# Sixteen plain steps on two tiles at a time, at the start of a Fourier-mixing and ELU kernel

## The chip, the cores and the metric

The kernel runs on one core of a Trainium2 chip. The metric is the device time of one execution in microseconds (us), as the median of several runs. A core has five engines that run side by side, each in the order of its own program: TensorE (PE, matrix products into PSUM; PEld is its loading of weights), VectorE (DVE), ScalarE (ACT), GpSimd (POOL) and SyncE (SP), which issues most of the DMA transfers. They wait for one another by semaphores.

## The reference

```
X = np.fft.fft(x, axis=1)            # x: (8, 3008, 256) float32
X = np.fft.fft(X, axis=2).real       # -> 24064 tokens x 256
h = X @ w_in                         # w_in: (256, 2048) float64
g = np.where(h > 0, h, np.exp(np.minimum(h, 0)) - 1)
out = (g @ w_out).astype(np.float32) # w_out: (2048, 256) float64
```

The weights reach the kernel as 64-bit words, and it makes 32-bit floats of them itself.

## The kernel before

**Transforms.** The Fourier transform over the 3008 positions is done as matrix products with cosine and sine matrices (`MC`), on sums and differences of four quarters of a batch (the folds, `fold_x`). `Dft` writes the results into rings of columns in SBUF: `Rr` and `Ir` for real and imaginary parts, `Rb` for one more channel, spread over all partitions. The second transform, over the 256 channels, is folded into the first weight matrix: `fold_chunk` multiplies 256 columns of w_in by channel matrices, `put_chunk` (ScalarE) copies the results to `Wc` and `Ws`, and `spread_last_row` sends one row of `Ws` through DRAM (`wx`, L392) and back as columns (`wex`, L394).

**Steps.** The main loop has 376 steps: 47 tiles of 256 columns, with 8 steps each. Step i takes 256 of the 2048 hidden features, those of chunk i % 8. `mm_P` makes the real part's product (tile `H`), `even_part` adds the extra channel with `wex` (tile `E`, VectorE, L713), `mm_Q` adds the imaginary part to `H`; `h_minus` makes 2E - H, the mirrored position; ScalarE and VectorE make the ELU of both (`G`, L723, L739). Two steps later the second product follows, into the accumulators pA to pD. In a plain step (`mm_plain`, the first 8) these are 8 matmul instructions. In all later steps they are 7, by a Winograd scheme: POOL makes four sums of blocks of `G` (`sum_1` to `sum_4`, L362), and four sums of weights (`WT`, `sum_weights`) take the place of part of the weights. At the end of a tile VectorE combines the accumulators (`COMB`), transposes them (L888, L895) and SyncE stores them (`store`, L927).

**Order.** All operations are written into a list of events with a time each (`at(t, fn)`, L1017; one slot is `PERIOD` = 4.8 in these units, called T). Sorted by these times, the list gives the order on the engines. The times are an order only: nothing is delayed until then. DMA issues aren't held to that order, so SyncE's order follows the scheduler. A transfer waits for the one issued eight places before it, by its semaphore.

**Start.** The weights are read in 8 chunks of w_in and 8 of w_out, 512 KB each (class `Chunk`). `load` brings the 64-bit words to a home in SBUF that something else uses later (`IN_HOMES`, `OUT_HOMES`: the homes of `WT`, parts of `Wc`, `Ws` and `w2`, `xl`, `rx`, `ot`). `fields` (VectorE) cuts out exponent and mantissa, `power` (ScalarE) makes the power of two in a temporary, `round` adds the two halves of the mantissa and `scale` multiplies. A chunk that is `shared` has the conversions on ScalarE (two more passes in `power`) and the addition and multiplication on POOL (`gtt`); the others do these on VectorE. In the kernel before, slots 0 to 4 have up to two chunks each, since step i needs chunk i of w_in from slot i on:

```
(w1_chunks[3], 0, 0), (w2_chunks[0], 0, 1), (w1_chunks[4], 1, 0),
(w2_chunks[1], 1, 1), (w1_chunks[5], 2, 0), (w2_chunks[2], 2, 1),
```

**The last channel.** One channel of all batches goes a way of its own: `load_ext` (L563) copies it from x in 16 parts, element by element; L580 writes rows to DRAM (`xe_dr`), `get_ext` (L586) reads them back (`xs`), `fold_ext` (POOL) folds them into `xe`, and `dft_ext` transforms them on TensorE, at slot 25 of the list. `dft_ext_0` and `ext_rows(1, gtt, 1)` do one part for batch 0 alone, earlier. `load_x(b)` (L144, L153, L154) loads a batch's four quarters, two of them by POOL.

Of the kernel before, what the change touches and what calls it, by code (L numbers as in the profile page):

```python
# [9 lines left out]
FP = mybir.dt.float32  # L10
BF = mybir.dt.bfloat16
U32 = mybir.dt.uint32
I32 = mybir.dt.int32
# [64 lines left out]
def kernel(  # L78
# [94 lines left out]
    class Chunk:  # L173
# [29 lines left out]
        def fields(self):  # L203

            if not wide:
                return
            lo, hi, dst = self.parts()
            if self.tmp_tag in ACC:
                t = bank(self.tmp_tag).bitcast(I32)
            else:  # L210
                t = spool.tile([128, 512], I32, tag=self.tmp_tag, bufs=1, name="pow2")
            self.t = t.rearrange("p (a b) -> p a b", a=dst.shape[1])
            pin(
                nc.vector.tensor_scalar(
                    out=self.t, in0=hi, scalar1=0x7FF00000, scalar2=None,
                    op0=ALU.bitwise_and,
                )
            )
            pin(
                nc.vector.tensor_scalar(  # L220
                    out=dst.bitcast(I32), in0=hi, scalar1=0xFFFFF, scalar2=0x100000,
                    op0=ALU.bitwise_and, op1=ALU.bitwise_or,
                )
            )
# [47 lines left out]
    def w1_dst(c):  # L272
        q, half = divmod(c, 2)
        if q not in w1:
# [3 lines left out]

    IN_HOMES = [(f"WT{c}", 1, 1024) for c in range(4)] + [
        Wc[:, 1024:2048],  # L280
        Ws[:, 1024:2048],
        ("xl0", 1, 6 * ND),
        ("xl1", 1, 6 * ND),
    ]
    OUT_HOMES = [w2[:, 1024 * (c + 1) : 1024 * (c + 2)] for c in range(3)] + [
        ("xl2", 1, 6 * ND),
        ("xl3", 1, 6 * ND),
        ("rx", 1, HALF + 1),
        ("ot", 2, 1024),
        ("ot", 2, 1024),  # L290
    ]
    ACC = ("pA", "pB", "pC", "pD")
    IN_TMP = ("u", "v", "u", "v", "pC", "pD", "pC", "pD")
    OUT_TMP = ("u", "v", "u", "v", "u", "pC", "pD", "pC")
    w1_chunks = [
        Chunk(
            moe_w_in[:, c * 256 : (c + 1) * 256].rearrange("(h p) n -> p h n", p=128),
            lambda c=c: w1_dst(c),
            IN_HOMES[c],
            IN_TMP[c],  # L300
            c in (1, 2, 3),
        )
        for c in range(8)
    ]
# [3 lines left out]
            lambda c=c: w2[:, c * 512 : (c + 1) * 512].rearrange("p (q n) -> p q n", q=2),  # L308
            OUT_HOMES[c],
            OUT_TMP[c],  # L310
            c < 5,
        )
        for c in range(8)
    ]
# [32 lines left out]
    def bank(tag):  # L347
        bufs = 3 if tag == "H" else 1
        return ppool.tile([128, 512], FP, tag=tag, bufs=bufs, name=tag)
# [14 lines left out]
    def act(o, i, func=AF.Copy, **kw):  # L364
        pin(nc.scalar.activation(out=o, in_=i, func=func, **kw))  # L365
# [440 lines left out]
    def mm_plain(i, a):  # L806

        S = steps[i]
        if i == 0 and a == 0:
            tiles[0] = Tile()  # L810
            tiles[0].acc = [bank(t) for t in ACC[0:2]]
        for n, (half, sign) in enumerate(((0, a), (1, 1 - a))):
            for r in range(2):
                mm(
                    tiles[0].acc[a][:, n * TW : (n + 1) * TW],
                    w2b(i, r, half),
                    blk(S, 2 * sign + r),
                    i == 0 and n == 0 and r == 0,
                    i == 7,
                )  # L820
        if a:
            del steps[i]
# [19 lines left out]
    def comb_copy(q):  # L842
        T = tiles[q]
        T.p1 = spool.tile([128, TW], FP, tag="p1", bufs=1, name="p1")
        act(T.p1, T.acc[0][:, 0:TW])

    def plain_u(q):
        T = tiles[q]
        T.u = spool.tile([128, 512], FP, tag="u", bufs=1, name="u")
        act(T.u, T.acc[0])  # L850

    def plain_v(q):
        T = tiles[q]
# [31 lines left out]
    def turn_u(q):  # L885
        T = tiles[q]
        T.o = spool.tile([128, 1024], FP, tag="ot", bufs=2, name="ot")
        pin(nc.vector.transpose(out=T.o[:, 0:512], in_=T.u))  # L888
        store(q, 0, 1, 0)
        store(q, 1, 0, 1)  # L890

    def turn_v(q):
        T = tiles.pop(q)
        tiles[q, 1] = T
        pin(nc.vector.transpose(out=T.o[:, 512:1024], in_=T.v))  # L895
        tiles[q] = T
        store(q, 2, 0, 0)
        store(q, 3, 1, 1)
        del tiles[q], tiles[q, 1]
# [126 lines left out]
    def load_rest():  # L1026

        ops["x1", 0]()
        act(MC[1, 0][0:1, 0:1], L_first[1][0:1, 0:1])
        load_mats(1, 0)  # L1030
        for chunk in (
            w1_chunks[2], w1_chunks[3], w2_chunks[0], w1_chunks[4], w2_chunks[1],
            w1_chunks[5], w2_chunks[5],
        ):
            chunk.load()

    at(-26.0, w1_chunks[0].fields)
# [8 lines left out]
    at(-24.8, lambda: fold_now("c2 e2 E2 o3 o2"))  # L1046
    at(-24.5, begin_x_even)
    at(-24.4, lambda: fold_now("c0 e0 c1 e1 E0 EO0"))
    at(-20.8, w2_chunks[2].load)
    for ri in (0, 1):  # L1050
        at(-20.7, lambda ri=ri: load_mats(ri, 1))
    at(-13.2, lambda: fold_chunk(0))
    at(-13.1, lambda: put_chunk(0))
    at(-13.0, lambda: dft_now(R_even, 1, "pA"))
# [16 lines left out]
    at(-10.5, lambda: dft_now(I_even, 0, "M"))  # L1071
    at(-10.4, w1_chunks[1].round)
    at(-10.3, w1_chunks[1].scale)
    at(0.95, w1_chunks[2].fields)
    at(0.96, w1_chunks[2].power)
    at(0.97, w1_chunks[2].round)
    at(1.7, w1_chunks[2].scale)
    at(1.3, lambda: fold_now("EO1"))
    at(3.9, lambda: fold_now("EO3"))
    at(-1.7, w1_chunks[6].load)  # L1080
    at(-1.6, w1_chunks[7].load)
    at(-1.5, w2_chunks[3].load)
    at(-1.4, w2_chunks[4].load)
    at(1.2, lambda: nc.sync.dma_start(out=pick, in_=PK_dr.ap()))

    T = PERIOD
    for chunk, k, second in (
        (w1_chunks[3], 0, 0),
        (w2_chunks[0], 0, 1),
        (w1_chunks[4], 1, 0),  # L1090
        (w2_chunks[1], 1, 1),
        (w1_chunks[5], 2, 0),
        (w2_chunks[2], 2, 1),
        (w1_chunks[6], 3, 0),
        (w2_chunks[3], 3, 1),
        (w1_chunks[7], 4, 0),
        (w2_chunks[4], 4, 1),
        (w2_chunks[5], 5, 1),
        (w2_chunks[6], 6, 1),
        (w2_chunks[7], 7, 1),  # L1100
    ):
        t = k * T + (1.9 if second and k == 0 else 1.0 if second or k == 0 else -0.5)
        at(t, chunk.fields)
        at(t + 0.02, chunk.power)
        at(t + 0.05, chunk.round)
        at(k * T + (3.7 if second else 1.7), chunk.scale)
    for c in range(1, 8):
        t = (c - 2) * T + 4.7 if c > 1 else 2.3
        at(t, lambda c=c: fold_chunk(c))
        t = (c - 1) * T + 1.4 if c > 1 else 3.0  # L1110
        at(t, lambda c=c: put_chunk(c))
        at(t + 0.01, lambda c=c: spread_last_row(c))
    for i in range(8):
        at((i + 3) * T + 1.0, lambda i=i: sum_weights(i))
    for c, k in ((5, 3.9), (6, 5.6), (7, 6.5)):
        at(k * T, w2_chunks[c].load)
    total = n_tiles * 8
    WINOGRAD = (
        (T + 2.91, sum_1),
# [3 lines left out]
        (2 * T + 0.87, mm_X1),  # L1123
        (2 * T + 3.04, mm_X2),
    )
    for i in range(total):
        t = i * T
        for dt, fn in (
            (0.0, mm_P),
            (0.9, even_part),  # L1130
            (2.17, mm_Q),
            (3.55, h_minus),
            (4.2, below_plus),
            (4.8, below_minus),
            (T + 1.5, exp_plus),
            (T + 2.2, g_plus),
            (T + 2.21, exp_minus),
            (T + 2.9, g_minus),
        ) + (
            (  # L1140
                (2 * T + 0.87, lambda i: mm_plain(i, 0)),
                (2 * T + 3.04, lambda i: mm_plain(i, 1)),
            )
            if i < 8
            else WINOGRAD
        ):
            at(t + dt, lambda fn=fn, i=i: fn(i))
# [4 lines left out]
        (T + 1.0, comb_22),  # L1152
        (T + 2.5, comb_3),
    )
    for q in range(n_tiles):
        t = (8 * q + 9) * T
        for dt, fn in (COMB if q else ((1.45, plain_u), (T + 1.1, plain_v))) + (
            (2 * T + 4.2 if q < n_tiles - 1 else T + 2.4, turn_u),
            (3 * T + 4.2, turn_v),
        ):  # L1160
            at(t + dt, lambda fn=fn, q=q: fn(q))
# [35 lines left out]
    for t, fn in (  # L1197
        (-1.8, I_even.copy),
        (0.0, I_even.plus),
        (0.1, I_even.minus),  # L1200
        (3.1, lambda: dft_now(R_odd, 1, "pA")),
        (3.2, lambda: dft_now(R_odd, 0, "pB")),
        (T + 0.95, R_odd.copy),
        (T + 1.0, R_odd.plus),
        (T + 1.1, R_odd.minus),
        (T + 3.1, lambda: dft_now(I_odd, 1, "pA")),
        (T + 3.2, lambda: dft_now(I_odd, 0, "pB")),
        (2 * T + 0.1, I_odd.copy),
        (2 * T + 0.2, I_odd.plus),
        (2 * T + 0.3, I_odd.minus),  # L1210
    ):
        at(t, fn)
    at(9 * T + 4.75, dft_ext_0)
    for g in (2, 3):
        at(10 * T + 1.46, lambda g=g: ext_side(g, 1))
    at(11 * T + 1.35, lambda: ext_rows(1, gtt, 1))
    at(11 * T + 2.0, lambda: spread_ext(0, 1))
    for n in range(16):
        j, k = divmod(n, 4)
        at(  # L1220
            (12 + 0.75 * n) * T,
            lambda j=j, k=k: load_ext(j, 192 * k, 192 * (k + 1)),
        )
    at(24.4 * T, get_ext)
# [8 lines left out]
    n_big = sum(k[0] not in "czx" for k, _ in fold_keys)  # L1233
    for b in range(1, NB):
        s0 = (b - 1) * steps_b
        l0 = s0 - 8 if b > 1 else 5.2
        at(l0 * T + 0.1, lambda b=b: state.update(L=load_x(b)))
        f0 = max(8, s0 - 1)
        f1 = s0 + 38
        at(f0 * T, lambda b=b: begin_folds(b))  # L1240
        n = 0
        for key in fold_keys:
# [64 lines left out]
```

## Time and profile before

| | |
|---|---|
| median of 6 runs | 1985.47 us (1984.92 to 1986.1) |
| profiled execution | 1995.33 us, span 1993.6 us |
| mean granted TensorE clock | 0.995 |
| busy: PE, PEld | 1960.8 us (98%), 1662.7 us (83%) |
| busy: DVE, ACT, POOL | 1281.0 (64%), 863.0 (43%), 1338.5 us (67%) |
| TensorE pauses before E, xe | 10.0 us (6 times), 7.9 us (once) |

The profile is that of one execution, and its time is longer than the median of the runs. "H<-Rr,Wc x4" is the first product of one step: each matmul instruction on 32-bit floats leaves two records. The line of most TensorE, ScalarE and POOL operations is that of a helper (L353, L365, L362), so they are told apart by their tiles.

### The profile page before, as it was taken

How to read it: one execution, taken by the hardware profiler on the slowest of the kernel's cores; microseconds unless marked ns; L12 is line 12 of the kernel's file. 1: busy time of each engine (PE TensorE's matmuls, PEld its weight loads, DVE VectorE, ACT ScalarE, POOL GpSimd, SP SyncE). 2: the span in 40 equal slices, each digit the busy share in tenths (PEclk: the TensorE clock that was granted, in tenths of full speed). 3: DMA queues.
4: the chain of work that ended last, by engine and by line, in shares of the span. 5: the costliest groups of instructions: out<-in, count | busy, mean ns of one | idle time of the engine just before them, and what ended most of it. 6: DMA issues, size and time to landing. Idle time of an engine off the chain costs nothing.

```text
span 1993.6 us, 26783 instructions
## 1 busy us (share of the span) xinstructions
PE 1960.8 (98%) x8880; PEld 1662.7 (83%) x8880; DVE 1281.0 (64%) x2340; ACT 863.0 (43%) x1654; POOL 1338.5 (67%) x1822
## 2 busy tenths in 40 slices
PE   8998999999999999999999999999999999999998
PEld 4787888888888888888888888888888888888887
DVE  7855656666566666666666665666656665566665
ACT  3543444444444434444434443444434444344443
POOL 3567757787477765777567775677757776455655
PEclk9999999999999999999999999999999999999999
DMA  8238301120001211011101211012010010100101
GB/s 320 85 20 21 87 11 17 28 75 16 15 15 37 59 23 17 14 49 44 26 14 19 59 28 28 12 19 83 12 21 12 19 21 15 17 12 12 22 10 23
DMA packets 256012, 71.61 MB, mean 36 GB/s; under 512 B 244271, under 2 KB 245060, under 8 KB 255362
## 3 DMA queue, kind: packets, MB, share of 16 engines
q1 hardware_dynamic: 251298, 57.05, 15.1%
q0 software_dynamic: 2400, 12.59, 2.0%
q8 instruction: 70, 1.15, 0.2%
q10 hardware_dynamic: 2176, 0.26, 0.1%
q14 instruction: 68, 0.56, 0.1%
HBM read 45.02 MB, written 24.80 MB: 35 GB/s over the span
## 4 chain that ended last, share of the span: by engine, by line
PE 90%; DMA 4%; DVE 2%; SPq 2%; ACT 1%; issue 1%; POOL 0%; DVEq 0%; POOLq 0%; ACTq 0%
PE H L353 36%; PE pB L353 15%; PE pD L353 15%; PE pC L353 15%; PE pA L353 8%; DMA x<-in_x_dram 2%; SPq L563 1%; DMA raw<-in_moe_w_in_dram 1%; DMA xl<-in_x_dram,ix 1%; DVE E L713 1%; DMA out_dram<-ot 0%; DMA wex<-wx 0%; DMA wx<-Ws 0%; SPq L927 0%; DVE G L739 0%
## 5 line engine op out<-in xcount | busy, mean ns | idle before, releaser
L362 POOL TENSOR_TENSOR G<-G 128x256 f32<-128x256 f32 x1472 | 1059.8, 729 | 580.3 <-DVE G L739 466.4
L713 DVE SCALAR_TENSOR_TENSOR E<-Rb,wex,H 128x256 f32<-128x256 f32 x752 | 327.9, 477 | 619.9 <-PE H L353 613.2
L365 ACT ACTIVATE G<-H 128x512 f32<-128x512 f32 x376 | 224.6, 597 | 949.0 <-DVE G L723 949.0
L353 PE MATMUL H<-Ir,Ws 128*128 128x256 f32 x1504 | 388.5, 381 | 10.1 <-DVE E L713 10.0
L353 PE MATMUL H<-Rr,Wc 128*128 128x256 f32 x1504 | 387.3, 380 | 0.7 <-ACT Wc L365 0.7
L353 PE MATMUL pC<-G,WT 128*128 128x256 f32 x1472 | 377.8, 379 | 0.0
L353 PEld LDWEIGHTS H<-Rr,Wc 128*128 128x128 f32 x1504 | 285.5, 190 | 55.0 <-issue 3.1
L353 PEld LDWEIGHTS H<-Ir,Ws 128*128 128x128 f32 x1504 | 277.7, 189 | 60.6 <-DVE E L713 13.4
L353 PEld LDWEIGHTS pC<-G,WT 128*128 128x128 f32 x1472 | 279.7, 190 | 38.0
L723 DVE SCALAR_TENSOR_TENSOR G<-E,H 128x512 f32<-128x512 f32 x376 | 257.4, 684 | 36.4 <-issue 0.6
L739 DVE SCALAR_TENSOR_TENSOR G<-G,H 128x512 f32<-128x512 f32 x376 | 256.2, 681 | 32.3 <-ACT G L365 32.2
L739 DVE SCALAR_TENSOR_TENSOR G<-M,G 128x512 f32<-128x512 f32 x376 | 257.3, 684 | 0.0
L353 PE MATMUL pB<-G,w 128*128 128x256 f32 x800 | 235.4, 381 | 0.0
L353 PE MATMUL pA<-G,w 128*128 128x256 f32 x800 | 234.0, 379 | 0.0
L365 ACT ACTIVATE G<-G 128x512 f32<-128x512 f32 x376 | 233.3, 620 | 0.0
L365 ACT ACTIVATE M<-G 128x512 f32<-128x512 f32 x376 | 224.0, 596 | 0.0
L365 ACT ACTIVATE M<-M 128x512 f32<-128x512 f32 x376 | 221.0, 588 | 0.1
L353 PE MATMUL pD<-G,WT 128*128 128x256 f32 x736 | 219.1, 379 | 1.6 <-DVE v L359 1.6
L353 PE MATMUL pB<-G,WT 128*128 128x256 f32 x736 | 219.3, 380 | 0.8 <-POOL G L362 0.8
L353 PE MATMUL pD<-G,w 128*128 128x256 f32 x736 | 218.9, 379 | 0.0
L353 PEld LDWEIGHTS pB<-G,w 128*128 128x128 f32 x800 | 152.7, 191 | 21.0
L353 PEld LDWEIGHTS pA<-G,w 128*128 128x128 f32 x800 | 152.1, 190 | 20.7
(139 smaller groups left out, 1335.3 us busy)
## 6 DMA issues: line engine op xcount, KB each, us to landing
out_dram<-ot SPq DMA_DIRECT2D x496, 32.0 KB
xl<-in_x_dram SPq DMA_DIRECT2D x16, 768.0 KB
MC<-dft_mats SPq DMA_DIRECT2D x4, 1131.0 KB
out_dram<-ot SPq DMA_DIRECT2D x256, 2.0 KB
Rb<-r SPq DMA_DIRECT2D x10, 376.0 KB
raw<-in_moe_w_in_dram SPq DMA_DIRECT2D x6, 512.0 KB
raw<-in_moe_w_out_dram SPq DMA_DIRECT2D x6, 512.0 KB
out_dram<-ot SPq DMA_DIRECT2D x64, 28.0 KB
```

The costliest lines, as they stand in the source:

```text
L353: nc.tensor.matmul(out_, lhsT=lhsT, rhs=rhs, start=start, stop=stop, skip_group_check=True)
L362: pin(nc.gpsimd.tensor_tensor(out=o, in0=a, in1=b, op=op))
L365: pin(nc.scalar.activation(out=o, in_=i, func=func, **kw))
L563: nc.sync.dma_start(out=t[:, s0:s1], in_=bass.AP(tensor=xt, offset=x.offset + row * ND + 128, ap=[[SEQ * ND, NB], [step * ND, s1 - s0], [1 ...
L713: nc.vector.scalar_tensor_tensor(out=S.E[:, c], in0=Rb[:, cols(i)], scalar=wex[:, f : f + 1], in1=S.H[:, c], op0=ALU.mult, op1=ALU.add,)
L723: nc.vector.scalar_tensor_tensor(out=two(S.G[:, 0:512])[:, :, ::-1], in0=two(S.E), scalar=2.0, in1=two(S.H), op0=ALU.mult, op1=ALU.subtract,)
L739: nc.vector.scalar_tensor_tensor(out=o, in0=e, scalar=-1.0, in1=h, op0=ALU.add, op1=ALU.max)
```

## The change

The first two tiles are taken side by side. Slot 0 does step 0 (tile 0), slot 1 step 8 (tile 1), slot 2 step 1, slot 3 step 9, and so on, up to slot 15; from slot 16 on, slot and step are the same again. Steps 8 to 15 become plain steps; their accumulators are pC and pD. Chunk c of w_in is now first used in slot 2c, and one chunk is converted per slot, in slots 0 to 12 and 14.

Further parts: all chunks but the first of w_in are shared (ScalarE and POOL in place of VectorE); the temporaries of the powers of two, part of them in pC and pD before, all lie in u and v; the homes `Ws`, `xl0` to `xl3` are replaced by `WT0` to `WT3`; the loads are put in another order and more of them later; the sums of weights move from slots 3 to 10 to slots 11 to 16; I_odd's transform moves from the accumulators' banks in slot 1 to H banks in slots 4 and 6; the last channel's early part and its copies move one slot later; tile 0's accumulators, and half of tile 1's, are transposed straight from PSUM, without a copy by ScalarE; batch 1 is loaded and folded on other slots.

```diff
-            if self.tmp_tag in ACC:
-                t = bank(self.tmp_tag).bitcast(I32)
-            else:
-                t = spool.tile([128, 512], I32, tag=self.tmp_tag, bufs=1, name="pow2")
+            t = spool.tile([128, 512], I32, tag=self.tmp_tag, bufs=1, name="pow2")
...
-        Ws[:, 1024:2048],
-        ("xl0", 1, 6 * ND),
-        ("xl1", 1, 6 * ND),
+        ("WT0", 1, 1024),
+        ("WT1", 1, 1024),
+        ("WT2", 1, 1024),
...
-        ("xl2", 1, 6 * ND),
-        ("xl3", 1, 6 * ND),
+        ("WT3", 1, 1024),
+        ("WT0", 1, 1024),
...
-    IN_TMP = ("u", "v", "u", "v", "pC", "pD", "pC", "pD")
-    OUT_TMP = ("u", "v", "u", "v", "u", "pC", "pD", "pC")
+    IN_TMP = "uvvuuuuu"
+    OUT_TMP = "uvvvvvuv"
...
-            c in (1, 2, 3),
+            c > 0,
...
-            c < 5,
+            True,
...
+        q = i // 8
+        if i % 8 == 0 and a == 0:
+            tiles[q] = Tile()
+            tiles[q].acc = [bank(t) for t in ACC[2 * q : 2 * q + 2]]
...
-        pin(nc.vector.transpose(out=T.o[:, 0:512], in_=T.u))
+        pin(nc.vector.transpose(out=T.o[:, 0:512], in_=T.u if q > 1 else T.acc[0]))
...
-        for chunk in (
-            w1_chunks[2], w1_chunks[3], w2_chunks[0], w1_chunks[4], w2_chunks[1],
-            w1_chunks[5], w2_chunks[5],
-        ):
+        w2_chunks[0].load()
+        w1_chunks[2].load()
+        load_mats(0, 1)
+        for chunk in (w1_chunks[3], w2_chunks[1], w1_chunks[4], w2_chunks[2]):
             chunk.load()
...
+        (w2_chunks[0], 0),
+        (w1_chunks[2], 1),
+        (w1_chunks[3], 2),
+        (w2_chunks[1], 3),
+        (w1_chunks[4], 4),
+        (w2_chunks[2], 5),
+        (w1_chunks[5], 6),
+        (w2_chunks[3], 7),
+        (w1_chunks[6], 8),
+        (w2_chunks[4], 9),
+        (w1_chunks[7], 10),
+        (w2_chunks[5], 11),
+        (w2_chunks[6], 12),
+        (w2_chunks[7], 14),
...
     for c in range(1, 8):
-        t = (c - 2) * T + 4.7 if c > 1 else 2.3
+        t = max(2 * c - 3, c % 3) * T + 4.7 if c > 1 else 2.3
         at(t, lambda c=c: fold_chunk(c))
-        t = (c - 1) * T + 1.4 if c > 1 else 3.0
+        t = max(2 * c - 2, 3) * T + 1.4 if c > 1 else 3.0
         at(t, lambda c=c: put_chunk(c))
...
-        at((i + 3) * T + 1.0, lambda i=i: sum_weights(i))
+        at((11 + 0.7 * i) * T + 1.0, lambda i=i: sum_weights(i))
...
-    for i in range(total):
-        t = i * T
+    for slot in range(total):
+        i = slot % 2 * 8 + slot // 2 if slot < 16 else slot
+        t = slot * T
...
-            if i < 8
+            if i < 16
...
+    at(17 * T + 1.0, lambda: turn_u(0))
+    at(17 * T + 4.2, lambda: turn_v(0))
+    at(18 * T + 1.0, lambda: turn_u(1))
+    at(18 * T + 1.45, lambda: plain_v(1))
+    at(19 * T + 4.2, lambda: turn_v(1))
+    for q in range(2, n_tiles):
...
-        (T + 3.1, lambda: dft_now(I_odd, 1, "pA")),
-        (T + 3.2, lambda: dft_now(I_odd, 0, "pB")),
...
+    at_half(4, lambda: I_odd, 1, 0)
+    at_half(6, lambda: I_odd, 0, HALF)
+    at(10 * T + 4.75, dft_ext_0)
...
-            (12 + 0.75 * n) * T,
+            (13 + 0.7 * n) * T,
...
-        l0 = s0 - 8 if b > 1 else 5.2
+        l0 = s0 - 8 if b > 1 else 7.2
...
-        f0 = max(8, s0 - 1)
-        f1 = s0 + 38
+        f0, f1 = (s0 - 1, s0 + 38) if b > 1 else (11, 37)
```

More of the change, by code (lines that the diff above doesn't have):

```diff
@@ L808, in mm_plain @@
         S = steps[i]
-        if i == 0 and a == 0:
-            tiles[0] = Tile()
-            tiles[0].acc = [bank(t) for t in ACC[0:2]]
+        q = i // 8
+        if i % 8 == 0 and a == 0:
+            tiles[q] = Tile()
+            tiles[q].acc = [bank(t) for t in ACC[2 * q : 2 * q + 2]]
         for n, (half, sign) in enumerate(((0, a), (1, 1 - a))):
@@ L814, in mm_plain @@
                 mm(
-                    tiles[0].acc[a][:, n * TW : (n + 1) * TW],
+                    tiles[q].acc[a][:, n * TW : (n + 1) * TW],
                     w2b(i, r, half),
                     blk(S, 2 * sign + r),
-                    i == 0 and n == 0 and r == 0,
-                    i == 7,
+                    i % 8 == 0 and n == 0 and r == 0,
+                    i % 8 == 7,
                 )
@@ L845, in comb_copy @@
         act(T.p1, T.acc[0][:, 0:TW])
[L847 to L850, printed above, removed]
     def plain_v(q):
@@ L894, in turn_v @@
         tiles[q, 1] = T
-        pin(nc.vector.transpose(out=T.o[:, 512:1024], in_=T.v))
+        pin(nc.vector.transpose(out=T.o[:, 512:1024], in_=T.v if q else T.acc[1]))
         tiles[q] = T
@@ L1048 @@
     at(-24.4, lambda: fold_now("c0 e0 c1 e1 E0 EO0"))
-    at(-20.8, w2_chunks[2].load)
-    for ri in (0, 1):
-        at(-20.7, lambda ri=ri: load_mats(ri, 1))
+    at(-20.7, lambda: load_mats(1, 1))
+    at(-20.6, w1_chunks[5].load)
+    at(-20.5, w2_chunks[5].load)
     at(-13.2, lambda: fold_chunk(0))
@@ L1073 @@
     at(-10.3, w1_chunks[1].scale)
[L1074 to L1077, printed above, removed]
     at(1.3, lambda: fold_now("EO1"))
[L1079 to L1083, printed above, removed]
     at(1.2, lambda: nc.sync.dma_start(out=pick, in_=PK_dr.ap()))
     T = PERIOD
[L1087 to L1100, printed above, removed]
+    for chunk, k in (
+        (w2_chunks[0], 0),
[12 more added lines that the diff above has]
+        (w2_chunks[7], 14),
     ):
-        t = k * T + (1.9 if second and k == 0 else 1.0 if second or k == 0 else -0.5)
+        t = k * T + 1.0
         at(t, chunk.fields)
@@ L1105 @@
         at(t + 0.05, chunk.round)
-        at(k * T + (3.7 if second else 1.7), chunk.scale)
+        at(k * T + (3.7 if k else 1.9), chunk.scale)
+    for chunk, t in (
+        (w1_chunks[6], 0.95),
+        (w1_chunks[7], 2.2),
+        (w2_chunks[3], 3.2),
+        (w2_chunks[4], 7.1),
+        (w2_chunks[6], 8.3),
+        (w2_chunks[7], 12.2),
+    ):
+        at(t * T, chunk.load)
     for c in range(1, 8):
-        t = (c - 2) * T + 4.7 if c > 1 else 2.3
+        t = max(2 * c - 3, c % 3) * T + 4.7 if c > 1 else 2.3
         at(t, lambda c=c: fold_chunk(c))
-        t = (c - 1) * T + 1.4 if c > 1 else 3.0
+        t = max(2 * c - 2, 3) * T + 1.4 if c > 1 else 3.0
         at(t, lambda c=c: put_chunk(c))
@@ L1113 @@
     for i in range(8):
-        at((i + 3) * T + 1.0, lambda i=i: sum_weights(i))
-    for c, k in ((5, 3.9), (6, 5.6), (7, 6.5)):
-        at(k * T, w2_chunks[c].load)
+        at((11 + 0.7 * i) * T + 1.0, lambda i=i: sum_weights(i))
+    at(2 * T + 4.2, lambda: fold_now("EO3"))
     total = n_tiles * 8
@@ L1154 @@
     )
-    for q in range(n_tiles):
+    at(17 * T + 1.0, lambda: turn_u(0))
[4 more added lines that the diff above has]
+    for q in range(2, n_tiles):
         t = (8 * q + 9) * T
-        for dt, fn in (COMB if q else ((1.45, plain_u), (T + 1.1, plain_v))) + (
+        for dt, fn in COMB + (
             (2 * T + 4.2 if q < n_tiles - 1 else T + 2.4, turn_u),
@@ L1205 @@
         (T + 1.1, R_odd.minus),
-        (T + 3.1, lambda: dft_now(I_odd, 1, "pA")),
-        (T + 3.2, lambda: dft_now(I_odd, 0, "pB")),
-        (2 * T + 0.1, I_odd.copy),
-        (2 * T + 0.2, I_odd.plus),
-        (2 * T + 0.3, I_odd.minus),
     ):
         at(t, fn)
-    at(9 * T + 4.75, dft_ext_0)
+    at_half(4, lambda: I_odd, 1, 0)
+    at_half(6, lambda: I_odd, 0, HALF)
+    at(10 * T + 4.75, dft_ext_0)
     for g in (2, 3):
-        at(10 * T + 1.46, lambda g=g: ext_side(g, 1))
-    at(11 * T + 1.35, lambda: ext_rows(1, gtt, 1))
-    at(11 * T + 2.0, lambda: spread_ext(0, 1))
+        at(11 * T + 1.46, lambda g=g: ext_side(g, 1))
+    at(12 * T + 1.35, lambda: ext_rows(1, gtt, 1))
+    at(12 * T + 2.0, lambda: spread_ext(0, 1))
     for n in range(16):
```

## The prediction, made before the changed kernel ran

> **What bounds the kernel now.** I read the page first: TensorE is busy for 98% of the span and the chain that ended last is 90% TensorE, at a clock of 0.995. So the time is TensorE's work plus its pauses. The second view is the list of what TensorE waited for over the whole run:
>
> ```profile
> PE H L353 <- DVE E L713: 10.0, 6, 3.5
> PE H L353 <- POOL xe L362: 7.9, 1, 7.9
> PE pA L353 <- DMA MC<-dft_mats: 1.9, 1, 1.9
> PE pD L353 <- DVE v L359: 1.6, 3, 0.5
> ```
>
> Columns: us in total, times, longest. Some 18 us go to two places: the even part E of the first steps, and one wait for `xe`. The third view, TensorE in order of time, places them:
>
> ```profile
> 45.63 2.07 PE L353 MATMUL H<-Ir,Ws 128*128 128x256 f32 x4 [3.51 <-DVE E L713]
> ...
> 74.85 1.13 PE L353 MATMUL H<-Ir,Ws 128*128 128x256 f32 x4 [2.74 <-DVE E L713]
> 75.82 3.25 PE L353 MATMUL pB<-G,w 128*128 128x256 f32 x8
> 78.86 2.27 PE L353 MATMUL H<-w,CC 128*128 128x256 f32 x8
> ...
> 112.46 1.13 PE L353 MATMUL H<-Rr,Wc 128*128 128x256 f32 x4
> ...
> 196.83 4.18 PE L353 MATMUL H<-MC,xe 128*8 128x377 f32 x24 [7.87 <-POOL xe L362]
> 200.94 1.88 PE L353 MATMUL H<-Rr,Wc 128*128 128x256 f32 x4
> ```
>
> Columns: start, length, work, pause before it. A slot runs from one first product (H<-Rr,Wc) to the next. 75.82 also shows a second price: that group takes 3.25 us, later ones 1.89, since the granted clock fell after the pause:
>
> ```profile
> 75.00:78.00 3.00, 3.00 (x10) 2.45 (x11) 2.21 (x4) 2.38 (x6) 1.47 (x3) 0.70 0.65 234
> ...
> 198.00:201.00 3.00, 3.00 (x21) 0.92 (x13) 0.00 (x0) 0.00 (x0) 2.78 (x4) 0.50 1.01 278
> ```
>
> (third number from the end: the clock). The fourth view is SyncE's queue:
>
> ```profile
> 129.32 2.35 SPq L563 DMA_DIRECT2D x<-in_x_dram  x2
> 131.79 7.53 SPq L927 DMA_DIRECT2D out_dram<-ot  x12
> 139.37 10.62 SPq L563 DMA_DIRECT2D x<-in_x_dram  x6
> ...
> 192.55 0.36 SPq L586 DMA_DIRECT2D xs<-xe_dr  x1
> 192.95 8.82 SPq L927 DMA_DIRECT2D out_dram<-ot  x16
> ```
>
> The copies of one channel (L563) come late because tile 0's stores (L927) stand ahead of them; `xs` lands at 194.78, POOL folds it, and TensorE, which was ready at 188.96, starts at 196.83.
>
> **The change part by part.**
>
> *Added products.* A full plain step has 12 matmul instructions, a Winograd step 11. One instruction of 256 columns is two records, and the start-to-start rows give 0.432 us (x8 records every 1.73 us). Steps 8 to 15 turn plain: 8 x 0.432 = 3.5 us more for TensorE.
>
> *Half the weight work per slot.* Before, slots 1 to 4 carry two chunks each; E starts at 44.70, 54.77, 63.88, 73.93 and 82.85, so 9 to 10 us per slot, with VectorE near full. With one chunk, in before's later slots, E starts at 82.85, 89.28, 95.70, 101.58: 6.4, 6.4, 5.9 us. After, one chunk per slot, rounded on ScalarE and POOL. Round trip by rows, start to start: two E 0.79, first field 0.33, three ScalarE passes 0.63+0.56+0.52, two copies of folded weights 0.54, exp 0.52, three G operations 1.8, sign 0.6: about 6.3 us with the copies, 5.8 without. TensorE's slot is 12 x 0.432 = 5.2, plus 1.73 with a chunk's fold or 1.9 with a DFT half: TensorE leads in most slots. I allow 1 us over slots 8, 12 and 14; the bounds are 0 and 4 (0.5 us a slot as the pauses of 0.50 and 0.42 us at 96.62 and 102.50 show).
>
> The powers of two move from PSUM to SBUF (tiles u, v). The two field rows take 0.75 us at 30.73 while POOL rests, but 1.80 us at 37.07 (1.47, then 0.41) while POOL runs 35.78 to 38.27.
> [...]
> [...]
>
> *The start.* By rows: P of slot 0 at 27.34, Q at 29.80, fold 1 from 30.74 to 32.5, as before. R_odd's matrix is now ahead of three weight loads and no longer waited for (1.87 us go): R_odd 32.5 to 36.3. Slot 1 (step 8, same weights): P, 0.87 for E, Q, to 39.0. P of slot 2 to 39.9. Products of step 0 need G, which stands on VectorE and ScalarE behind chunk 2's fields and passes: 42.1 to 43.8. Q of slot 2 needs the last row of chunk 1 (wx, then wex). Before wx, 14.9 MB are issued (six w_in and four w_out chunks, the matrices, batch 0, and now batch 1's two gathers); at before's 0.4 MB per us this ends near 39.4. Before wex go one chunk and a 0.8 MB load: 3.3 us, and 2 for itself: 44.7. E 0.9, Q 0.9, products 1.7, fold 2 1.7: slot 3 at 49.9; I add 1 for the clock, so **51** (bounds 49.9 and 53.7, where before had its slot 2). Chunk 0's own wex now stands behind a gather on POOL's queue: 0 to 1 us, hidden by that later wait.
>
> *Slots 3 to 17.* 15 x 5.18 + five folds 8.7 + I_odd 3.8 + `dft_ext_0` 2.0 = 92.2: slot 18 at 143.2 plus 1 for round trips. Before: 112.46 + 8 x 4.75 = 150.5. On POOL the sums of weights now lie in slots 11 to 17, against 0.46 to 0.74 us each: with chunks, folds and ext rows 36 us stand ahead of the first Winograd sums, due 39 us after slot 11 begins, and these take 3: 0 to 3 us late, I take 1. TensorE would reach `dft_ext` at 143.2 + 1 + 1 + 38 = 183.2. Transposing from PSUM instead of SBUF is not in the trace: VectorE's 0.69 from PSUM against 0.42 for a field bounds the four at plus 1.1 us, and the ScalarE copies taken away give 0.6 back there; VectorE has room, so 0.
>
> *The copies for `dft_ext`.* The program's order on SyncE has all 16 now ahead of the stores of tiles 0 and 1. They start behind the small rows of POOL in slot 12. Slot 12 begins at 51 + 9 x 5.18 + 8.7 + 3.8 + 2.0 + 1 = 113. POOL has 8.5 us from slot 11 and then a round, a fold and 1.9 us of rows: 8.3 us into slot 12; two DMAs (121.74 to 123.6 before) make it 10.2, so 123.3. Before, 14 copies ran from 139.4 to about 190.6 (xs then took 4.2 more): 3.64 us each. 16 x 3.64 + 4.2 = 62.5: 185.8. POOL's 2.05 (194.78 to 196.83): **`dft_ext` at 187.9 against 196.83, 8.9 us earlier**, after a pause of 4.7. If the copies ran at the busy share alone (46 of 51 us, 3.2 us each), the pause would be gone and TensorE's 183.2 would rule: 13.6 earlier, and 2.9 more if the clock doesn't fall (4.11 us for `dft_ext` against some 2.05 at full clock, 0.85 in the next products). The other end: slot 3 at 53.7, POOL 2 later: 4.2 earlier.
>
> The pause of 7.87 shows a clock of 0.50, the one of 2.74 still 0.70. [...] I keep the loss.
>
> *Behind it.* 40 stores stand behind the copies: 24 of tile 0 at 0.47 to 0.63 us, 11 to 15 us after 183.6, plus 3.9 to land: 199 to 203. The transpose of tile 2 needs that buffer at about 187.9 + 4.1 + 0.9 + 4.75 + 4 = 201.7. On VectorE the next E stands behind it. 0 to 1.5 us, with 1 us of slack: 0.
>
> **Sum:** 8.9 us of 1995.33 in the profiled execution (span 1993.6), 1986.4; the median of the runs is 9.9 lower, so 1976.6. All later slots are equal.
>
> **The rivals.**
> 1. *Copies no longer last.* The clean end above: 13.6 to 16.5 earlier, 1969 to 1972. For it: busy share under 1; against: the queue drains at each of the four row writes.
> 2. *The start gets later instead.* DMA, not VectorE, sets slot 2, and batch 1's loads (768 KB, 2 us each) now stand in that queue: with two or three of them more ahead of wex, slot 3 comes at 55 to 60, the pairs relieve nothing there, and the rest keeps 0 to 5 us, 1980.5 to 1985.5. For it: the 42 us during which the DMA share is about 1.
> [...]
>
> **How the numbers follow.** Forecast 56% (1971 to 1981), rival 1 17%, rival 2 16%, rival 3 11%. About 0.2%, 4 us, is what a measurement can tell from no change. Faster by more: 56 + 17 + 6 = 79%. Same: the rest of rival 2, 10%. Slower: 11%. The range 1968 to 1982 leaves out rival 3 and most of rival 2.
>
> **What would show it.** Slot 3 near 51 and slot 18 near 145; no pause over 1 us at E from slot 4 on; the first one-channel copy near 123, ahead of all stores; `dft_ext` near 188 with a pause of 3 to 6 us and a fallen clock. Wrong if E starts more than 7.9 us apart, or if a copy takes over 4 us.

## The result, and the profile after

The changed kernel takes **1988.63 us** (median of 16 runs, 1987.10 to 1994.42) beside 1985.09 us for the kernel before (37 runs, 1983.31 to 1992.34). The ratio is 1.0021, with a 95% interval of 1.0015 to 1.0028: slower by 0.21%, where 8.9 us less had been forecast (1976.6, range 1968 to 1982). The profiled execution took 1988.94 us, with a span of 1987.2 us at a mean clock of 0.998. Some executions of a kernel, with no change in the program, come out 3 to 10 us above the rest, and the profiled execution of the kernel before, at 1995.33 us, was one of these.

Three places of the trace tell the story. The list of what TensorE waited for, over the whole run of the changed kernel (us in total, times, longest):

```profile
PE pA L350 <- POOL w L359: 6.1, 5, 1.6
PE H L350 <- DVE E L710: 3.3, 4, 1.4
PE pA L350 <- DVE G L736: 2.1, 1, 2.1
...
PE H L350 <- POOL xe L359: 0.3, 1, 0.3
```

The two large entries of before have shrunk: E from 10.0 to 3.3 us, `xe` from 7.9 to 0.3. But a new one leads, which before did not have: five waits for `w`, the converted weights of w_out, from POOL. TensorE in order of time places them (start, length, work, pause ahead of it):

```profile
51.77 1.03 PE L350 MATMUL H<-Rr,Wc 128*128 128x256 f32 x4
...
60.91 1.99 PE L350 MATMUL pA<-G,w 128*128 128x256 f32 x8 [1.21 <-POOL w L359]
...
76.21 1.99 PE L350 MATMUL pA<-G,w 128*128 128x256 f32 x8 [1.05 <-POOL w L359]
...
91.14 1.99 PE L350 MATMUL pA<-G,w 128*128 128x256 f32 x8 [0.68 <-POOL w L359]
...
105.15 1.99 PE L350 MATMUL pA<-G,w 128*128 128x256 f32 x8 [1.65 <-POOL w L359]
...
121.58 1.99 PE L350 MATMUL pA<-G,w 128*128 128x256 f32 x8 [1.54 <-POOL w L359]
...
153.09 1.03 PE L350 MATMUL H<-Rr,Wc 128*128 128x256 f32 x4
...
191.52 2.32 PE L350 MATMUL H<-MC,xe 128*8 128x377 f32 x24 [0.28 <-POOL xe L359]
```

Slot 3 begins at 51.77, as worked out (51). Slot 18 begins at 153.09, where 145.2 had been worked out, and in between stand five pauses, 14 to 16 us apart, one in every second slot. `dft_ext` starts at 191.52 with hardly a pause. The third place is why `w` is late, in the order of time of VectorE and POOL around the first of the five:

```profile
55.95 1.30 POOL L359 TENSOR_TENSOR w<-w 128x512 f32<-128x512 f32 x1 [2.44 <-ACT w L362]
...
56.96 0.69 DVE L736 SCALAR_TENSOR_TENSOR G<-G,H 128x512 f32<-128x512 f32 x1 [2.58 <-ACT G L362]
57.57 0.68 DVE L736 SCALAR_TENSOR_TENSOR G<-M,G 128x512 f32<-128x512 f32 x1
58.17 0.68 DVE L720 SCALAR_TENSOR_TENSOR G<-E,H 128x512 f32<-128x512 f32 x1
...
58.76 0.69 DVE L254 SCALAR_TENSOR_TENSOR pow<-w,pow 128x512 int32<-128x512 int32 x1
...
59.59 1.26 POOL L359 TENSOR_TENSOR w<-w,pow 128x512 f32<-128x512 f32 x1 [2.34 <-DVE pow L254]
```

A chunk's last two operations are the sign on VectorE (L254, `pow<-w,pow`) and the multiplication on POOL (`w<-w,pow`); the list gives both the due time 3.7 of the slot. POOL's addition was done at 57.25. The sign had its inputs too (ScalarE's power was done at 54.80), but it stood on VectorE behind the G operations and 2E - H, in the list's order. So it came at 58.76, POOL rested 2.34 us and ended at 60.85, and TensorE, ready at 59.70, began at 60.91. Chunks 1 to 5 of w_out are converted in slot 2c + 1 and used at the start of slot 2c + 2: that deadline is missed all five times.

**An ordinary execution of the kernel before.** A second profile of the unchanged kernel (below as b_again) took 1985.17 us, close to the median of the runs (1985.09). TensorE's waits, first:

```profile
PE H L353 <- DVE E L713: 10.2, 6, 3.5
PE H L353 <- ACT Wc L365: 1.9, 1, 1.9
...
```

(five smaller entries follow, none of them `xe`), and its `dft_ext` in order of time:

```profile
189.55 2.09 PE L353 MATMUL H<-MC,xe 128*8 128x377 f32 x24
```

There is **no wait for `xe`**, and `dft_ext` takes 2.09 us in place of 4.18. The 7.87 us, the largest term of the forecast, are not there in this execution. What differs is the speed of the copies. SyncE's queue in b_again:

```profile
138.69 8.83 SPq L563 DMA_DIRECT2D x<-in_x_dram  x6
...
179.94 0.36 SPq L586 DMA_DIRECT2D xs<-xe_dr  x1
```

The six copies begin at the same place as before (138.69, then 139.37), but they take 8.83 us against 10.62, and the last `xs` is issued at 179.94 instead of 192.55.

### The profile page after: what moved, and what is told of

The parts are those of the page before. It is cut to its first block, busy times and chain, and to the rows that moved or that the text cites. A ratio compares the mean times of both kernels' runs of the same rounds, so it can differ in the third digit from the quotient of the medians.

```text
span 1987.2 us, 26822 instructions
## 1 busy us (share of the span) xinstructions
PE 1960.9 (99%) x8896; PEld 1662.9 (84%) x8896; DVE 1263.4 (64%) x2322; ACT 869.6 (44%) x1666; POOL 1329.6 (67%) x1804
## 4 chain that ended last, share of the span: by engine, by line
PE 91%; DMA 3%; DVE 2%; SPq 2%; ACT 1%; POOL 1%; issue 1%; POOLq 0%; DVEq 0%; ACTq 0%
PE H L350 37%; PE pB L350 15%; PE pD L350 15%; PE pC L350 15%; PE pA L350 8%; SPq L560 1%; DMA x<-in_x_dram 1%; DMA raw<-in_moe_w_in_dram 1%; DMA xl<-in_x_dram,ix 1%; DVE E L710 0%; POOL w L359 0%; SPq L577 0%; DVE G L720 0%; POOL G L359 0%; ACT pow L362 0%
## 5 line engine op out<-in xcount | busy, mean ns | idle before, releaser
L359 POOL TENSOR_TENSOR G<-G 128x256 f32<-128x256 f32 x1440 | 1034.8, 728 | 564.7 <-DVE G L736 454.0
L350 PE MATMUL pC<-G,WT 128*128 128x256 f32 x1440 | 369.5, 379 | 0.0
L350 PEld LDWEIGHTS pC<-G,WT 128*128 128x128 f32 x1440 | 273.6, 190 | 37.2
L350 PE MATMUL pB<-G,w 128*128 128x256 f32 x784 | 229.5, 379 | 0.0
L350 PE MATMUL pD<-G,w 128*128 128x256 f32 x784 | 229.2, 379 | 0.0
L350 PE MATMUL pB<-G,WT 128*128 128x256 f32 x720 | 214.5, 380 | 1.6 <-POOL G L359 1.6
L350 PE MATMUL pD<-G,WT 128*128 128x256 f32 x720 | 214.4, 379 | 1.6 <-DVE v L356 1.6
```

The lines of the kernel that those rows point to most:

```text
L350: nc.tensor.matmul(out_, lhsT=lhsT, rhs=rhs, start=start, stop=stop, skip_group_check=True)
L359: pin(nc.gpsimd.tensor_tensor(out=o, in0=a, in1=b, op=op))
```

## The experiments

Two theories stood after the result. **A**: (1) the wait for `xe` is in some executions only, so the median held little of it to win; and (2) the new pauses of 6.1 us, with 3.5 us of added products, take back what the better start gives. **B**: the wait for `xe` is always there, the change removed it as forecast, and the plain steps or the later part of the run cost some 12 us. The kernels ran in three groups, each on one chip beside runs of the kernel before: b_again, b_ext_late, a_scale_early and a_drop_one (before: median 1985.36 us, 11 of 35 above 1990 us); b_scale_early, a_sign_mid, b_more_copies and a_again (1985.63, 7 of 35); a_scale_again, a_wex_pool and a_start (1987.79, 7 of 25). The ratios compare means, so they count these executions; where they matter, the medians are given too.

**b_again: the kernel before, unchanged, with a profile.**

> The kernel before, unchanged, for a second profiled execution. Theory A (the pause of 7.87 us for xe, with some 2.9 us of half clock behind it, belongs to the one profiled execution and not to the ordinary ones): time equal to the other runs of before, and if this profile has no such pause, its own time is near 1985 instead of 1995. Rival B (the pause is in every execution): the profile shows 6 to 9 us of pause for xe again, and its time is within 2 us of the ordinary runs once what the profile itself adds is taken off.

Measured: 1985.49 us (1984.23 to 1995.12), 2 of 10 above 1990; its profile is the one shown above. With two profiles of one program, one with the wait and 10.2 us longer, one without it, the first half of A holds for these two executions; the next run tests it on more.

**b_ext_late: the kernel before, with `dft_ext` six slots later.**

```diff
-    at(24.4 * T, get_ext)
-    at(25 * T + 1.35, fold_ext)
-    at(25 * T + 4.75, dft_ext)
+    at(30.4 * T, get_ext)
+    at(31 * T + 1.35, fold_ext)
+    at(31 * T + 4.75, dft_ext)
...
-            step = s0 + (28, 38)[kodd]
+            step = s0 + (35 if b == 1 else 28, 38)[kodd]
```

(the uses of the result move by six or seven slots too).

> The kernel before with the last channel's reading back, fold, transform and rows six slots later (slot 31 in place of 25), so that nothing waits for its copies. Theory A: ordinary runs within 2 us of before, about 1985. Rival B: 8 to 11 us faster, about 1975, the forecast's own gain.

Measured: 1985.21 us (1984.53 to 1987.57), ratio 0.9985 (0.997 to 0.9999). The median is that of the kernel before, 1985.36, and none of 12 executions lies above 1987.57, where 11 of 35 of the kernel before lay above 1990.7 on the same chip. Six slots, some 28 us, of room for the copies change nothing in the median and take the long executions away: the wait for `xe` is theirs alone, and B falls.

**b_more_copies: the kernel before, with four of the 16 copies made twice.**

```diff
-    for n in range(16):
+    for n in (0, 1, 2, 3, *range(16)):
```

> The kernel before with four of the sixteen one-channel copies made twice, and one row write more. It lengthens the chain of copies in every execution by 4 x 2.77 = 11 us. By the second profile of before, xe could have been 5.2 us later at no cost, so theory A: a pause for xe of about 6 us and 1 to 3 us of half clock behind it, 7 to 9 us slower than before, 1992 to 1994, which is also where the single late executions of before lie. Rival (the late executions have another cause, and the chain has much room in ordinary ones): 0 to 3 us slower.

Measured: 1992.97 us (1990.03 to 2003.20), ratio 1.004 (1.0021 to 1.0058), as A had it. TensorE in order of time, in its profiled execution of 1990.03 us:

```profile
192.88 3.57 PE L353 MATMUL H<-MC,xe 128*8 128x377 f32 x24 [3.85 <-POOL xe L362]
```

With four more copies and a row, all ten executions lie above 1990 us, and the profiled one, the shortest of them, has the wait. So in an ordinary execution of before, the copies end a few us ahead of need: the chain that the prediction took for the bound has slack there.

**a_scale_early: the change, with sign and multiplication (`scale`) moved up to where the chunk's fields are cut out, from 3.7 of the slot's 4.8 units to 1.06 (t is 1.0 in each slot).**

```diff
-        at(k * T + (3.7 if k else 1.9), chunk.scale)
+        at(t + 0.06, chunk.scale)
```

> The changed kernel with each chunk's sign operation right behind its fields on VectorE, ahead of the G operations. Theory A: the five pauses of pA for POOL's weights, 6.1 us together, go; 4 to 6 us faster than the changed kernel, 1982.5 to 1984.5, a little under before. Rival B: the copies for xe end last in ordinary runs too, and start only 3 us earlier; 0 to 3 us faster, 1986 to 1988.6.

Measured: **1980.75 us** (1979.87 to 1988.33), ratio 0.9968 (0.9953 to 0.9982): 7.9 us less than the change (6.7 less than a_again below) and 4.6 less than before. The same place in order of time of VectorE and POOL:

```profile
53.41 0.69 DVE L254 SCALAR_TENSOR_TENSOR pow<-w,pow 128x512 int32<-128x512 int32 x1 [0.46 <-ACT pow L362]
54.55 1.30 POOL L359 TENSOR_TENSOR w<-w 128x512 f32<-128x512 f32 x1 [3.85 <-ACT w L362]
55.56 0.69 DVE L736 SCALAR_TENSOR_TENSOR G<-G,H 128x512 f32<-128x512 f32 x1 [1.46 <-ACT G L362]
55.92 1.27 POOL L359 TENSOR_TENSOR w<-w,pow 128x512 f32<-128x512 f32 x1
```

The sign now stands ahead of G, and POOL's multiplication follows its addition at once and ends at 57.19. TensorE:

```profile
57.16 1.03 PE L350 MATMUL H<-Rr,Wc 128*128 128x256 f32 x4
58.02 1.89 PE L350 MATMUL pA<-G,w 128*128 128x256 f32 x8
...
144.80 1.03 PE L350 MATMUL H<-Rr,Wc 128*128 128x256 f32 x4
...
182.88 2.09 PE L350 MATMUL H<-MC,xe 128*8 128x377 f32 x24
```

No pause ahead of pA; slot 18 at 144.80 and `dft_ext` at 182.88, where the prediction had 145.2 and 183.2 for TensorE on its own. A repeat beside two later kernels:

> The kernel of a_scale_early once more, beside the next two on one chip. Theory A (the pauses for POOL's w are gone and nothing takes their place): 1980.75 again, 1979.9 to 1981.7, 0.23% below the kernel before. Rival (the 4.6 us were an accident of one chip): a ratio that reaches 1.

Measured: 1980.50 us (1979.92 to 1981.82, 8 runs), ratio 0.9965 (0.9951 to 0.9979).

**a_sign_mid: the change, with the same two operations at 3.3 in place of 3.7, ahead of 2E - H alone.**

> The changed kernel with the sign operation moved only a little: ahead of the 2E - H operation (0.6 us on VectorE), still behind the two G operations. A dose for the pauses of pA. Theory A (sign, then POOL's product of 1.27 us, ends last before pA): each of the five pauses is 0.6 us shorter, 2.5 to 3 us in all; 3 us faster than the changed kernel, 1985.5. Rival (the addition on POOL or ScalarE's passes end last): no change of the pauses, 1988.5.

Measured: 1985.24 us (1984.66 to 1991.17), ratio 0.9994 (0.998 to 1.0007). Beside a_again, on the same chip, the pauses for `w` fall from 6.5 us to

```profile
PE pA L350 <- POOL w L359: 3.4, 4, 1.5
```

and the median by 2.2 us, from 1987.45. A part of the cure gives a part of the gain: the time follows the pauses.

**b_scale_early: the same edit in the kernel before.** It tells whether the edit is good by itself, or only mends what the change did.

```diff
-        at(k * T + (3.7 if second else 1.7), chunk.scale)
+        at(t + 0.06, chunk.scale)
```

> The kernel before with the same edit that made the changed kernel fast: each chunk's sign operation right behind its fields. It asks whether that edit alone, without the pairs, does the work. Theory A (pairs and early sign are needed together; before has no pause for POOL's weights): within 3 us of before. Rival: the edit gains by itself, 4 us or more faster than before, 1981 or less.

Measured: 1988.12 us (1986.17 to 1996.97), ratio 1.0015 (1.0 to 1.003). There it costs 2.5 us of median, with an interval that just reaches 1. With two chunks a slot, the earlier signs push VectorE's fold of the first batch back (it starts at 34.11 and takes 2.04 us, against 31.40 and 0.95 in the first profile of the kernel before), and TensorE waits for it:

```profile
PE pA L353 <- DVE e L426: 3.7, 1, 3.7
```

So the gain of a_scale_early is that of the change with its missed deadline mended, not of a habit that helps anywhere.

**a_drop_one: the change, with one of the eight second products of steps 8 to 15 left out** (so tile 1 lacks an eighth of its second products), to price the added products.

```diff
-            for r in range(2):
+            for r in range(1 if q and a and n else 2):
```

> The changed kernel with one of the 8 second-product instructions of steps 8 to 15 left out, so its output isn't the reference's. It measures the price of plain against Winograd steps on TensorE. Theory A: 8 x 0.432 = 3.5 us faster than the changed kernel, 1985.1, about the same as before. Rival B: what is taken ahead of the copies' end is lost again there, 0 to 2 us faster.

Measured: 1987.68 us, but spread evenly from 1984.93 to 1994.70 over 12 runs; ratio 1.0004 (0.9987 to 1.0021). Its shortest execution is 2.2 us under the shortest of the change (1987.10). In its profile the pauses for `w` are 7.4 us, 1.3 more than in the change: TensorE, with less to do, waits longer for the same multiplication. It can't price the products well, and why its runs spread so is open.

**a_again: the change, unchanged, with a second profile.**

> The changed kernel, unchanged, for a second profiled execution. Theory A: five pauses of pA for POOL's weights, 6 to 7 us together, as in the first; xe early, without a pause if the copies run at 2.8 us each as in the second profile of before; time 1987 to 1989 in most runs. Rival: the pauses differ from execution to execution and cannot carry the loss.

Measured: 1987.45 us (1987.24 to 1987.98, 10 runs) beside 1985.63 for the kernel before (medians, 1.8 us apart); the ratio of means is 0.9998 (0.9982 to 1.0014), since that of before holds its seven long executions. The pauses for `w` are 6.5 us, and `dft_ext` starts at 190.18 without a pause. The change is slower by 1.8 to 3.5 us of median; by the means, this one chip shows no difference.

**a_wex_pool and a_start: a_scale_early, and the wait of slot 2 attacked.** In a_wex_pool chunk 1's last row goes by POOL's queue; in a_start, besides, the power, rounding and scaling of the chunk in slot 1 are put behind G.

```diff
-        queue = nc.sync if q else nc.gpsimd
+        queue = nc.sync if q > 1 else nc.gpsimd
```

```diff
-        at(t + 0.02, chunk.power)
-        at(t + 0.05, chunk.round)
-        at(t + 0.06, chunk.scale)
+        late = 1.3 if k == 1 else 0.0
+        at(t + 0.02 + late, chunk.power)
+        at(t + 0.05 + late, chunk.round)
+        at(t + 0.06 + 1.6 * late, chunk.scale)
```

> The same with chunk 1's last row sent by POOL's queue, where fewer loads stand ahead of it than on SyncE's. What sets slot 2? In a_scale_early slot 2 begins at 39.88 and slot 3 at 50.25, 10.4 us for some 8 of work; E of slot 2, at 44.90, waits 1.43 us for the DMA of wex. Theory A (the wex transfer sets slot 2): E there comes 1 to 1.4 us earlier, slot 3 at about 49, and the time is 1979.5. Rival (the products of step 0 set it, 2.12 us late by VectorE's G, and the queue is as full on POOL's side): slot 3 within 0.4 us of 50.25 and the time 1980.75.

> As a_wex_pool, and in slot 1 the conversion of the next chunk of w_in moved behind the exp and the G of step 0 on ScalarE and VectorE. In a_scale_early the products of step 0 wait 2.12 us for that G at 43.03. Theory A (G stands behind the chunk's passes): the pause at 43 is under 0.5 us and with the earlier wex slot 3 begins at about 47.5, the time is 1978. Rival (the chunk, now later, is missed by the fold of slot 3 or 4): the pause comes back there, as a wait for POOL's w or for the folded weights, and the time is 1980.75 or more.

Measured: a_wex_pool 1982.36 us (1980.84 to 1987.37), ratio 0.9974 (0.9963 to 0.9986); a_start 1984.48 (1982.53 to 1992.67), ratio 0.9989 (0.9974 to 1.0004). Both miss: they are 1.9 and 4.0 us slower than a_scale_again on the same chip. POOL and VectorE of a_wex_pool in order of time:

```profile
40.27 0.76 POOL L391 DMA_DIRECT2D wex<-wx  x1 [4.60 <-DMA wx<-Ws]
...
45.99 0.87 DVE L710 SCALAR_TENSOR_TENSOR E<-Rb,wex,H 128x256 f32<-128x256 f32 x2 [2.81 <-DMA wex<-wx]
```

The row was written at 35.10 and the read back issued at 40.27 on POOL; on SyncE, in a_scale_again, these were 33.25 and 39.93, and E came at 44.58. So E is 1.4 us later, not earlier. From 43 to 46 us the DMA share is 0.99, with 370 GB/s moved, so loads filled the DMA engines while the row was under way. What sets the row's time is not shown: in a_scale_again the share is 0.94 and E came 1.4 us earlier. In a_start the pause of 2.12 us for G did fall, to 0.88, but TensorE then waited 3.16 us for the E that needs `wex`, at 46.97: the one pause had covered the other, and the clock from 46 to 49 us, where this longer single pause ends, was 0.50 (1.00 in a_wex_pool, with pauses of 2.12 and 2.22 us). Its profiled execution, 1990.66 us, had the wait for `xe` again, 4.57 us. `wex` bounds slot 2 and stays unmended.

## Why the prediction was wrong, by its own steps

1. **The main failure: the sum's base, "8.9 us of 1995.33 in the profiled execution".** The step took its gain from a wait that belongs to the long executions. The one number that spoke against it was in the table: the profiled execution was 9.9 us above the median. A pause of 7.87 us and a loss of clock of 2.9 (10.8 together) is about that difference; the prediction instead carried the same 9.9 us over to the new kernel as a constant. In an ordinary execution `dft_ext` started at 189.55 without a pause, so TensorE's own work was the bound there, and the most that a start 6.3 us better (TensorE at 183.2) can give is some 6 us. Where the wait is, the step nearly holds: both first profiles have slow copies, and there the change is 6.4 us faster (1995.33 to 1988.94, one execution each). By size the next step misses more (6.1 to 6.5 us against 8.9 - 6.3 = 2.6), and it took both to turn the gain into a loss: with the wait and the pauses the change gains 6.4 us, with neither 4.6 (a_scale_early).
2. **The second failure: "TensorE leads in most slots ... I allow 1 us" for the round trips, with bounds of 0 and 4.** What it cost is 6.1 to 6.5 us. The sum of the work per slot was no cause: slots 3 to 11 have the time. The step added up the round trip of VectorE and ScalarE, and its sum has no term for POOL's two operations (1.30 and 1.26 us in the rows above). That a chunk has a deadline (sign, then POOL's multiplication, then pA) stands in none of its terms, and the listed order put these two operations behind G. From slot 3 to slot 18 the prediction had 94.2 us; a_scale_early takes 94.6, the change 101.3 and 101.9. The 7 us between them are the five pauses and little else. In slots 3 to 11 of the change E starts 6.5 to 9.2 us apart, three times of eight over the limit of 7.9 that the prediction's last line sets (8.55, 8.39 and 9.23), and the pauses stand in each second slot.
3. **The start: right.** Slot 3 at 51.77 and 50.19 in the two profiles (51 forecast); rival 2 didn't come. No pause for E exceeds 1 us from slot 4 on.
4. **The copies: their order right, their start late.** They ran ahead of all stores, from 130.36 and 129.37 (123.3 forecast; 124.24 in a_scale_early, without the pauses). In the profiled execution a copy took some 3.5 us by the prediction's own measure (3.64 there), and `xs` landed just in time; in a_again they took some 2.8. Rival 1, "copies no longer last", is what ordinary executions do, before the change as well as after it; so its gain of 13.6 to 16.5 us, worked out against the same pause, is not there either.
5. **Added products, 3.5 us.** Not priced by themselves (a_drop_one couldn't). The account leaves room for them: from the first product to `dft_ext`, b_again takes 161.7 us with 12.8 us of pauses, a_again 163.0 with 11.7. That is 2.4 us more beside the pauses, while the mean clock of that stretch went from 0.97 to 0.99, worth up to 3.3 us (0.02 x 163) the other way.
6. **"All later slots are equal": wrong by some 1.4 us.** `dft_ext` is 0.6 us later in a_again than in b_again, the span 2.1 longer. In a_again TensorE waits 1.09 us at 212.19 for POOL's G, a wait that b_again doesn't have there: in a_again POOL has an indirect load of `xl` (0.97 us at 208.94) ahead of those sums. The rest was not traced further.
7. **The 40 stores behind the copies, and the transposes from PSUM: 0, as costed.** TensorE's list shows no wait for the stores, and a transpose takes 0.71 us from PSUM as from SBUF (0.70).

Put right, the forecast would have been: a start worth 6.3 us, less 1.4 behind it, is 4.9 us under 1985.1, 1980.2, where a_scale_early measured 1980.75 and 1980.50; five missed deadlines, 6.1 to 6.5 us, make it 1986.5, where the change measured 1987.45 and 1988.63. One to two us of the change stay without a name; in the first profile 1.2 us more than in a_again is a longer wait for a DFT matrix at the start (1.8 against 0.6).

## What to carry to other kernels

Compare the profiled execution's time with the median before taking a gain from one of its waits: a wait as large as the difference may be missing from the ordinary runs. Where work is moved nearer to its use, add up latencies along the chain to the deadline, in the order in which each engine holds them, and not only busy times per slot. And look for the second wait under the one that is to be removed.

## What the runs showed of the hardware

- **A copy's speed changed between executions of one program.** The one-channel copies (L563 before, L560 after) took some 3.6 and 3.5 us each in the first profiles of the two kernels, and about 2.8 in the second ones. From the six copies shown to the last `xs` issued it is 53.2 us in before and 41.2 in b_again; from the first copy on, 58.0 in the change and 47.3 in a_again. In the three profiles of the last group, on another chip, it is 55.7 to 60.3, and there the median of before is 2 us higher. What decides the speed is open. In the kernel before, the long executions go with the wait for these copies: with `dft_ext` six slots later (b_ext_late), none of 12 lies above 1987.57 us.
- **The clock after a pause of 2.1 us fell in some executions and not in others.** TensorE's rows after the same wait for G, and the busy time of the stretch from 43 to 46 us (third number from the end: the clock), in a_again:

```profile
42.20 3.39 PE L350 MATMUL pA<-G,w 128*128 128x256 f32 x8 [2.11 <-DVE G L736]
```

```profile
43.00:46.00 3.00, 3.00 (x8) 1.92 (x7) 1.58 (x5) 0.86 (x3) 1.26 (x1) 0.50 0.89 332
```

and in a_scale_early:

```profile
43.03 1.97 PE L350 MATMUL pA<-G,w 128*128 128x256 f32 x8 [2.12 <-DVE G L736]
```

```profile
43.00:46.00 3.00, 2.13 (x9) 1.60 (x10) 1.57 (x4) 1.09 (x2) 0.76 (x1) 1.00 0.96 374
```

The group after the same pause took 1.4 us more in the one than in the other. In six profiles with this pause (each has another of 0.96 or 0.97 us, which ends 2 us of work ahead of it), the group took 2.52 us (the change), 2.62 (a_scale_again) and 3.39 (a_again), but 1.97 (a_scale_early, a_drop_one) and 1.96 (a_wex_pool). What decides between them is not shown.
- **One of VectorE's signs took 1.83 us beside a POOL operation.** In a_start it started at 41.62, beside POOL's addition of 41.58 to 42.89:

```profile
41.58 1.31 POOL L359 TENSOR_TENSOR w<-raw,w 128x512 f32<-128x512 f32 x1
```

```profile
41.62 1.83 DVE L254 SCALAR_TENSOR_TENSOR pow<-raw,pow 128x512 int32<-128x512 int32 x1
```

It ended 0.56 us after POOL's operation; what held it is not shown. In the change, 14 of 16 signs took 0.68 or 0.69 us (the longest 1.39). In slots 3 to 11 its fields and signs together took 1.6 us more than at their shortest, so a lengthening like that of the prediction's two field rows (0.75 us and 1.80) came to little here.
